# Seven first products of the feed-forward's first row group run as fill of the last attention group, with their Mish behind the seam

## The chip, the cores and the metric

The kernel runs on one core of one Trainium2 chip. The metric is the time of one execution in device microseconds; of the kernel before there are three runs, 677.23, 675.67 and 678.56 us, with 677.23 us as the median. In this document PE is TensorE's matmuls, PEld its weight loads, DVE is VectorE, ACT is ScalarE, POOL is GpSimd, and SP is the queue that issues all DMAs of this kernel.

## What is computed

One transformer block with adaptive layer norm on one sequence of 2048 rows: sliding-window attention (16 heads of 28 columns, a window of 256), then a two-layer feed-forward with Mish between its layers. Everything is in float32.

```python
B, S, D, F, H, W = 1, 2048, 448, 1792, 16, 256
mod = (silu(c) @ w_mod).reshape(c.shape[0], 6, 1, -1)
sa, ca, ga, sb, cb, gb = (mod[:, i] for i in range(6))
h = layernorm(x) * (1 + ca) + sa
q, k, v = heads(h @ wqkv)
p = softmax(where(0 <= i - j < W, q @ k.T * 28 ** -0.5, -1e9))
x = x + ga * ((p @ v) @ wo)
h = layernorm(x) * (1 + cb) + sb
x = x + gb * (mish(h @ w1 + b1) @ w2)
```

## The kernel before

**Split operands.** A float32 factor is kept as a high part, rounded for the fast matmul format, and a low part, the rest. A product of two such factors is three matmuls for each 128 rows of the contraction: high by high, high by low, low by high. With 448 rows (three chunks of 128 and one of 64, which holds its own low part in the other 64 partitions) one product of the first layer is 11 matmuls (`passes`, L205). ACT makes a high part as a copy, DVE or POOL the low part as a difference.

**Row groups.** The 2048 rows are four groups of 512. The attention runs over 4 groups x 16 heads x 3 blocks of the band, 192 steps `u` of the loop at L1109, so steps 144 to 191 are the last group. A step issues B(u): on PE the scores of one head and block into one of two PSUM banks `sB` (after a bfloat16 matmul, L759, that adds the mask, unless ACT has put the mask there ahead of time, L739, a "seed"), and on ACT their exponential `P` (L734). Every fourth step issues `pv`, 16 narrow matmuls (L769). Most steps also issue a scan of the scores of a later head, `sA` on PE with a masked maximum `junk` on DVE (L687, L689), up to step 179.

**Fill.** The order of the work on every engine is the order of the program text; nothing reorders it. So each step also pulls other work from generators and issues it between the attention's own: `fill_main(g)` (L994) by a credit of RATE[g] per step against a cost for each piece of matmul work, and one `side_step` per step from `fill_late` (in the last group: `gen_w1`, L841). Evictions of such work are put in `pipe` and issued one or two steps later. In the last group the fill was the output projection of the group before (`gen_oT`, then `gen_wo`: 44 matmuls `wo`), and then the second layer norm of row group 0 (`gen_ln2_0`: four ACT normalisations `x`, 16 transposes `trf`, four evictions `hhf` on ACT and their low parts on DVE). RATE was 0.45. `gen_w1` loaded and split 4 of the 16 pieces of W1. When the steps are over, the generators are drained (L1152).

**The seam and the feed-forward.** At steps 192 to 195 (`TAIL`) the first two products z0 and z1 of the feed-forward start beside the last `pv`, and ACT loads the table that holds Mish. Then the loop at L1213 goes over 4 row groups x 14 column blocks, n = 0 to 55. Loop n issues `f1_mm(n)` (11 matmuls `z`, L970), `f1_act(n)` (on ACT Mish `t` and its high part `ah`, on DVE its low part `al`, L976 to L978), in row group 0 `pieces(n)` (ACT and POOL split the n-th piece of W2 into `w2h` and `w2l`, and pieces of W1), and `ff2(n - 1)` (12 matmuls `acc`, L1177 to L1179, of which every third needs `al`). In row group 0 four `fill_step`s per loop issue the rest of the attention's work: transposes and projection of the last group (`ot`, `wo`, with DVE's additions `xr`) and the second layer norm of row group 1, whose 64 transposes run on DVE (`yt`, L897, four blocks of 16). z14, the first product of row group 1, needs all of them. `ah` and `al` have two buffers each.

Of the kernel before, what the change touches and what calls it, by code (L numbers as in the profile page):

```python
# [51 lines left out]
def adaln_block(ctx: ExitStack, tc: tile.TileContext, x, wqkv, wo, w1, b1, w2, c, w_mod, out):  # L52
# [582 lines left out]
    def gen_wo(g, tag, bufs):  # L635
        oh, ol = OT[g]

        def add(xr, p, t):
            DVE.tensor_tensor(xr, xr, p[:, 0:D], op=ALU.add)
            ln_stats(xr, mv2[g][:, t, :], cst, f"w{g}{t}")  # L640

        xrs = XR[g]

        def store(xr, t):
            j = 4 * g + t
            dma(x1d[j * 128:(j + 1) * 128, :], xr)
            if t == 0:
                later.append(lambda: xr_load(g, 3))

        for t in range(4):  # L650
            j = 4 * g + t
            if t not in xrs:
                flush()
            xr = xrs[t]
# [25 lines left out]
    def A(i, t):  # L680
# [5 lines left out]
        p = bank("mm" if i >= 60 and t % 2 else "sA", 2, f"sA{i}_{t}")  # L686
# [115 lines left out]
    FW = {}  # L802
# [6 lines left out]

    def w2_dma(f):  # L810
        w2p[f] = load_piece(w2[f * 128:(f + 1) * 128, :], 0, 0, D, stage(f"w2p{f}"))
# [23 lines left out]
    SEQ = [e for f in range(NF) for e in [("w2", f)] + [("w1", n) for n in (2 * f + 4, 2 * f + 5) if n < len(W1)]]  # L835
# [5 lines left out]
    def gen_w1():  # L841
# [12 lines left out]
        w1_load(0)  # L854
        for n in range(1, 4):
            yield
            yield
            w1_load(n)
        yield "bank"
        b1c = FW["b1c"] = p1.tile([128, NF], F32, name="b1c")  # L860
        p = bank("mm", 2, "b1t")
        PE.transpose(p[:, 0:NF], b1r, ident[0:NF, 0:NF])
        ACT.activation(b1c, p[:, 0:NF], AF.Copy)
        x1_load(0, p1)
# [6 lines left out]
        yield "bank"  # L871
        pb = bank("mm", 2, "gb")
# [3 lines left out]
        yield  # L876
# [27 lines left out]
    XN2 = {}  # L904

    def gen_ln2(g, pl, xn_tiles, tag, bufs):
        xs = None
        for r in gen_ln([x1[g][:, t, 0:D] for t in range(4)], pl, xn_tiles, f"f{g}", g == 0, mv=mv2[g]):
# [5 lines left out]
        if g:  # L914
            yield from ln2_blocks(g, xs, hh, hl)
            return
        for ci in range(4):
            p = bank(tag, bufs, f"trf{g}{ci}")
            tr_chunk(xs, ci, p)
            pipe.add(2, lambda p=p, ci=ci: hT_hi(p, ci, hh, 2), lambda p=p, ci=ci: hT_lo(p, ci, hh, hl, 2))  # L920
            yield
            yield

    def gen_ln2_0():
        p1 = FW["p1"]

        yield from gen_ln2(0, p1, lambda: [x1[0][:, t] for t in range(4)], "mm", 2)
        yield from finish()
        for i in range(4):
            piece_load(i)  # L930
            yield
# [10 lines left out]
    def pieces(f):  # L942
        for i, (kind, n) in enumerate(SEQ):
            if kind == "w2" and n == f:
                w2_split(n)
            elif kind == "w1" and (n - 4) // 2 == f:
                w1_hi(n)
                w1_lo(n, DVE if f < 1 else POOL)
            else:
                continue  # L950
# [9 lines left out]
    zb = {}  # L960

    def f1_mm(n, tag, part=(0, 11)):
        g, f = divmod(n, NF)
        hh, hl = h2[g]
        fs = slice(f * 128, (f + 1) * 128)
        if part[0] == 0:
            zb[n] = bank(tag, 2, f"z{n}")
        ps = passes(hh, hl, FW["w13"][:, :, fs], FW["w1l"][:, :, fs])
# [3 lines left out]
    def f1_act(n):  # L972
        f = n % NF
        ah[n], al[n] = ftile("ah", n, F32R), ftile("al", n, F32R)
        t = ftile("t", n)
        ACT.activation(t, zb[n], AF.Mish, bias=FW["b1c"][:, f:f + 1])  # L976
# [17 lines left out]
    def fill_main(g):  # L994
# [21 lines left out]
        if g + 1 == NG:  # L1016
            yield from finish()
            yield from gen_ln2_0()

# [29 lines left out]
    RATE = (0.76, 1.01, 0.88, 0.45)  # L1049
# [139 lines left out]
    def gen_x1_ln2(g):  # L1189
        if g > 1:  # L1190
            x1_load(g, (ff, p1)[g % 2])
# [9 lines left out]
    x1_load(0, ff)  # L1201
    for i in range(4, 9):
        piece_load(i)
    x1_load(1, p1)
# [8 lines left out]
    for n in range(NN + 1):  # L1213
        g, f = divmod(n, NF)
        if f == 0 and n:
# [42 lines left out]
```

## Time and profile before

| What | Value |
|---|---|
| Median of the three runs | 677.23 us |
| Lowest, highest | 675.67, 678.56 us |
| Span of the profiled execution, first to last instruction | 674.8 us |
| ACT busy over the span | 336.9 us (50%) |
| POOL busy over the span | 120.9 us (18%) |
| Mean granted TensorE clock of the span | 0.990 |

The profile gives no other time for the profiled execution than its span, which lies 0.9 us under the lowest of the three runs and 2.4 us under their median. Times in the trace are microseconds from the start of the span. The matmuls of the trace overlap (each record of 512 columns is about 0.4 us long, while the next one starts 0.23 us later), so a busy PE is not a full PE: the distance of one start from the next tells what a matmul costs, and the weight loads, one for each matmul of 128 columns of weights, show the pace.

### The profile page before, as it was taken

The numbers are of one execution on the slowest core, as the hardware profiler recorded it, in microseconds if no ns is written. First come the engines' busy times: TensorE is split into PE (matmuls) and PEld (weight loads), VectorE is DVE, ScalarE is ACT, GpSimd is POOL, SyncE is SP. The second block draws the span as 40 slices with busy tenths as digits, with TensorE's granted clock in tenths as the row PEclk, the third lists the DMA queues.
The fourth block names the chain that finished last, engine by engine and source line by source line (L and its number), as shares of the span: only waits on it lengthen the run. The fifth ranks groups of instructions, "written<-read, shape, count | busy, mean of one in ns | idle before, by whom it ended". The sixth has DMA issues, their size and how long they took to land.

```text
span 674.8 us, 10729 instructions
## 1 busy us (share of the span) xinstructions
PE 637.9 (95%) x3712; PEld 511.0 (76%) x3712; DVE 391.7 (58%) x1138; ACT 336.9 (50%) x584; POOL 120.9 (18%) x173
## 2 busy tenths in 40 slices
PE   4998999899999999998989999989999999999996
PEld 3876676577887678776666788878888888888885
DVE  6865676756677767567767333963485438631112
ACT  4554566678765677734667743442333323322221
POOL 6741010233011100000030245431012001100002
PEclk9999999999999999997999999999999999999999
DMA  8875775456855478434772654003000300010001
GB/s 227 225 234 191 263 260 159 134 149 197 279 138 156 140 220 289 144 107 113 192 217 63 220 162 137 14 1 110 0 1 0 109 2 0 1 54 1 1 0 54
DMA packets 49169, 83.77 MB, mean 124 GB/s; under 512 B 5838, under 2 KB 27612, under 8 KB 49116
## 3 DMA queue, kind: packets, MB, share of 16 engines
q1 hardware_dynamic: 49116, 83.10, 40.3%
q8 instruction: 29, 0.48, 0.3%
q14 instruction: 24, 0.20, 0.1%
HBM read 53.45 MB, written 29.36 MB: 123 GB/s over the span
## 4 chain that ended last, share of the span: by engine, by line
PE 66%; DVE 15%; issue 12%; DMA 3%; ACT 2%; POOL 1%; SPq 0%; POOLq 0%; DVEq 0%; ACTq 0%
PE z L970 15%; PE qk L321 8%; DVE junk L689 6%; PE sA L687 6%; PE pv L769 6%; PE sB L731 5%; PE acc L1179 4%; PE acc L1178 4%; PE acc L1177 4%; PE wo L321 3%; PE qk_v L321 3%; DVE yt L897 3%; PE sB L759 2%; DMA k<-scr 1%; PE qk L506 1%
## 5 line engine op out<-in xcount | busy, mean ns | idle before, releaser
L689 DVE CUSTOM_DVE_ANT_0 junk<-sA,strip 128x384 bf16<-128x384 f32 (+2 forms) x256 | 135.7, 530 | 91.6 <-PE sA L687 76.7
L734 ACT ACTIVATE P<-sB 128x512 f32<-128x512 f32 (+2 forms) x192 | 108.6, 571 | 99.1 <-PE sB L731 96.7
L978 DVE TENSOR_TENSOR al<-t,ah 128x512 fp32r<-128x512 f32 x56 | 41.2, 736 | 137.2 <-ACT ah L977 136.8
L976 ACT ACTIVATE t<-z,b1c 128x512 f32<-128x512 f32 x56 | 38.4, 686 | 156.8 <-PE z L970 145.8
L687 PE MATMUL sA<-k,q 84*128 84x384 f32 (+2 forms) x256 | 93.5, 370 | 10.7 <-DVE mx L689 6.2
L970 PE MATMUL z<-hhf,w 128*128 128x512 f32 x224 | 89.0, 397 | 0.0
L970 PE MATMUL z<-hlf,w 128*128 128x512 f32 x224 | 88.8, 396 | 0.0
L731 PE MATMUL sB<-q,k 86*128 86x384 f32 (+1 forms) x352 | 84.9, 316 | 0.0
L1179 PE MATMUL acc<-w2h,al 128*128 128x448 f32 x224 | 82.1, 366 | 1.9 <-DVE al L978 1.9
L1177 PE MATMUL acc<-w2h,ah 128*128 128x448 f32 x224 | 81.9, 366 | 0.0
L1178 PE MATMUL acc<-w2l,ah 128*128 128x448 f32 x224 | 81.8, 365 | 0.0
L731 PEld LDWEIGHTS sB<-q,k 86*128 86x128 f32 x352 | 59.4, 193 | 13.1 <-issue 5.1
L970 PE MATMUL z<-hhf,w1l 128*128 128x512 f32 x168 | 66.5, 396 | 0.0
L687 PEld LDWEIGHTS sA<-k,q 84*128 84x128 f32 x256 | 48.3, 191 | 23.2 <-DVE mx L689 15.1
L897 DVE STREAM_TRANSPOSE yt<-xn 32x128 f32<-32x128 f32 x192 | 58.1, 302 | 2.6
L739 ACT ACTIVATE sB<-strip 128x512 f32<-128x512 bf16 (+2 forms) x95 | 54.6, 575 | 3.0
L769 PE MATMUL pv<-P,v 128*32 128x256 f32 (+2 forms) x704 | 50.6, 402 | 0.0
L970 PEld LDWEIGHTS z<-hlf,w 128*128 128x128 f32 x224 | 42.1, 188 | 10.1
L970 PEld LDWEIGHTS z<-hhf,w 128*128 128x128 f32 x224 | 42.1, 188 | 9.1 <-issue 0.6
L1179 PEld LDWEIGHTS acc<-w2h,al 128*128 128x128 f32 x224 | 42.1, 188 | 5.9 <-DVE al L978 2.6
L1177 PEld LDWEIGHTS acc<-w2h,ah 128*128 128x128 f32 x224 | 42.1, 188 | 5.0
L1178 PEld LDWEIGHTS acc<-w2l,ah 128*128 128x128 f32 x224 | 42.1, 188 | 4.8
(155 smaller groups left out, 1024.2 us busy)
## 6 DMA issues: line engine op xcount, KB each, us to landing
k<-scr SPq DMA_DIRECT2D x48, 252.0 KB
q<-scr SPq DMA_DIRECT2D x64, 168.0 KB
scr<-st SPq DMA_DIRECT2D x21, 512.0 KB
scr<-st SPq DMA_DIRECT2D x29, 256.0 KB
x<-x1d SPq DMA_DIRECT2D x10, 448.0 KB
xin<-in_A_x_dram SPq DMA_DIRECT2D x8, 448.0 KB
xr<-in_A_x_dram SPq DMA_DIRECT2D x16, 224.0 KB
x1d<-xr SPq DMA_DIRECT2D x16, 224.0 KB
```

Source lines behind the costliest of these rows:

```text
L321: PE.matmul(p, b, a, start=(n == 0), stop=(n == 10))
L687: PE.matmul(p[:, c0:384], q[0:84, t * 128:(t + 1) * 128], k[0:84, t * 128 + c0:t * 128 + 384], start=True, stop=True)
L689: DVE.tensor_tensor_reduce(out=junk[:, c0:384], in0=p[:, c0:384], in1=mask[:, c0:384], scale=1.0, scalar=-3.0e38, op0=ALU.add, op1=ALU.max ...
L731: PE.matmul(p[:, c:c + 128 * (t1 - t0)], k[:, jj * 128:(jj + 1) * 128], q[:, t0 * 128:t1 * 128], start=False, stop=True, skip_group_check= ...
L734: ACT.activation(P[:, c0:], p[:, c0:], AF.Exp, scale=SCALE)
L739: ACT.activation(p[:, c0:], strip[:, c + c0:c + 512], AF.Copy)
L769: PE.matmul(pvb[q][32 * a:32 * a + 32, t0 * 128:t1 * 128], V[j % NV][:, h + a, :], Pt[4 * w + a][:, c:c + 128 * (t1 - t0)], start=(b == 0 ...
L897: DVE.transpose(y4[32 * j:32 * j + 32, ci, :, 32 * i:32 * i + 32], x4[32 * i:32 * i + 32, :, ci, 32 * j:32 * j + 32])
L970: PE.matmul(zb[n], ps[m][1], ps[m][0], start=(m == 0), stop=(m == 10))
L1177: PE.matmul(p, ah[n][:, ts], w2h[f], start=(f == 0), stop=False)
L1178: PE.matmul(p, ah[n][:, ts], w2l[f], start=False, stop=False)
L1179: PE.matmul(p, al[n][:, ts], w2h[f], start=False, stop=(f == NF - 1))
```

## The change

z2 to z8, the products of seven column blocks of row group 0, leave the feed-forward's loop and become the last item of the last attention group's fill (`gen_f1`). Their sums are moved from PSUM to SBUF by ACT, with the bias added (`z_out`), into three tiles `zs` of the tag `xr` and four slices `zx` of the tag `x1`. Behind the seam `f1_act` takes Mish in place from there. So that their operands are ready, W1's pieces 0 to 11 (before: 0 to 3) are loaded and split inside the last attention group, and the layer norm of row group 0 is done by `gen_w1` between those pieces instead of after the projection. The column blocks are taken in the order FO. RATE of the last group goes from 0.45 to 0.80. The last heads' scan uses two banks `sA` where it had four. Loads of the last group's `x` rows (`xr`) move behind the Mish that frees their buffers, and row group 0's residual `x1` is loaded a second time at loop n = 9.

```diff
-            if ci < 3:
+            if ci < 3 and g < NG - 1:
                 later.append(lambda t=ci: xr_load(g, t))
...
-        p = bank("mm" if i >= 60 and t % 2 else "sA", 2, f"sA{i}_{t}")
+        p = bank("sA", 2, f"sA{i}_{t}")
...
+    ZT = 2
+    ZN = 9
+    FO = (7, 8, 0, 1, 2, 3, 4, 5, 6, 9, 10, 11, 12, 13)
...
-    SEQ = [e for f in range(NF) for e in [("w2", f)] + [("w1", n) for n in (2 * f + 4, 2 * f + 5) if n < len(W1)]]
+    w1_cols = [0]
+    SEQ = [e for f in range(NF) for e in [("w2", f)] + [("w1", n) for n in (f + 11,) if 12 <= n < len(W1)]]
...
+        x1_load(0, p1)
+        for n in range(3):
             w1_load(n)
+            yield
+        ln = gen_ln([x1[0][:, t, 0:D] for t in range(4)], p1, lambda: [x1[0][:, t] for t in range(4)], "f0", True,
+                    mv=mv2[0])
...
-        for n in range(4):
+        for n in range(12):
+            next(ln, None)
             yield
             w1_hi(n)
-            yield "dve"
             w1_lo(n, POOL)
+            if n % 4 == 3:
+                w1_cols[0] += D
+            next(ln, None)
+            yield
+            if n == 2:
+                XN2[0] = [x1[0][:, t] for t in range(4)]
+            if n + 3 < 12:
+                later.append(lambda n=n: w1_load(n + 3))
...
+    def z_out(n, p):
+        if n < ZT + 3:
+            zs[n] = xr_tile(f"zs{n}")
+        else:
+            if n == ZT + 3:
+                FW["zx"] = FW["p1"].tile([128, 4, GT], F32, name="zx", tag="x1")
+            zs[n] = FW["zx"][:, n - ZT - 3]
+        f = FO[n]
+        ACT.activation(zs[n], p, AF.Identity, bias=FW["b1c"][:, f:f + 1])
...
+    def gen_f1():
+        for n in range(ZT, ZN):
+            while w1_cols[0] < 128 * (FO[n] + 1):
+                yield
+            p = bank("mm", 2, f"z{n}")
+            w = yield from tile_mms(p, f1_passes(n))
+            pipe.add(2, lambda n=n, p=p: z_out(n, p))
+            yield w
+        yield from finish()
...
-        t = ftile("t", n)
-        ACT.activation(t, zb[n], AF.Mish, bias=FW["b1c"][:, f:f + 1])
+        if n in zs:
+            t = zs[n]
+            ACT.activation(t, t, AF.Mish)
+        else:
+            t = ftile("t", n)
+            ACT.activation(t, zb[n], AF.Mish, bias=FW["b1c"][:, f:f + 1])
...
             yield from gen_ln2_0()
+            yield from gen_f1()
...
-    RATE = (0.76, 1.01, 0.88, 0.45)
+    RATE = (0.76, 1.01, 0.88, 0.80)
...
-    x1_load(0, ff)
+    x1_load(1, ff)
...
+        if n == ZN:
+            x1_load(0, p1)
...
-            f1_mm(n, "z")
+            if n not in zs:
+                f1_mm(n, "z")
             f1_act(n)
+        if n - ZT in (0, 1, 2):
+            xr_load(NG - 1, n - ZT)
```

**PE, attention step 183 to 184.** In the order of PE's instructions before, the step's fill is one group of transposes (`sB183` and `sB184` are the scores of steps 183 and 184, `et14` a transpose of the attention's output):

```order
L731 MATMUL sB183_4518<-q2_3_393,k3_7_381 128x384
L731 MATMUL sB183_4518<-q2_3_393,k3_7_381 128x128
L780 MATMUL et14_4525<-ident_127,o4_14_4491 128x128 x4
L254 MATMUL trf01_4530<-ident_127,x1_0_4150 128x128 x4
L759 LDWEIGHTS identr_136
L759 MATMUL sB184_4536<-strip_138,identr_136 128x256
```

In the order of the change, the same place on PE:

```order
L733 MATMUL sB183_4616<-q2_3_393,k3_7_381 128x384
L733 MATMUL sB183_4616<-q2_3_393,k3_7_381 128x128
L782 MATMUL et14_4623<-ident_127,o4_14_4591 128x128 x4
L321 MATMUL z5_4578<-hlf0_4257,w13_4008 128x512
L321 MATMUL z5_4578<-hhf0_4256,w13_4008 128x512
L321 MATMUL z5_4578<-hlf0_4257,w13_4008 128x512
L321 MATMUL z6_4631<-hhf0_4256,w13_4008 128x512
L321 MATMUL z6_4631<-hhf0_4256,w1l_4009 128x512
L761 LDWEIGHTS identr_136
L761 MATMUL sB184_4637<-strip_138,identr_136 128x256
```

The transposes are gone from here (they stand at steps 165 to 169 now), and five matmuls of z5 and z6 stand in their place. In the whole order of the change, steps 171 to 190 hold 70 of the 77 moved matmuls and step 191 the last 7; `wo` stands at 32 matmuls in steps 152 to 159 (19 before) and at 12 in steps 160 to 162 (25 in steps 160 to 171 before).

**ACT, attention steps 160 to 163.** Before, ACT's order holds the exponentials `P`, the seeds `sB` and, from step 163 on, a split of W1 (`w13`):

```order
L734 ACTIVATE P160_4082<-sB160_4049 128x512
L739 ACTIVATE sB162_4084<-strip_138 128x512
L734 ACTIVATE P161_4115<-sB161_4111 128x512
L734 ACTIVATE P162_4136<-sB162_4084 128x512
L739 ACTIVATE sB164_4138<-strip_138 128x512
L863 ACTIVATE b1c_4146<-b1t_4147 128x14
L734 ACTIVATE P163_4161<-sB163_4157 128x512
L186 ACTIVATE w13_3996<-w1p0_4000 128x448
```

In the change, the same steps on ACT:

```order
L736 ACTIVATE P160_4118<-sB160_4070 128x512
L741 ACTIVATE sB162_4120<-strip_138 128x512
L240 ACTIVATE x1_0_4012<-x1_0_4012,nmf0_4113,rsf0_4085 128x448
L736 ACTIVATE P161_4162<-sB161_4158 128x512
L186 ACTIVATE w13_4008<-w1p1_4028 128x448
L240 ACTIVATE x1_0_4012<-x1_0_4012,nmf0_4113,rsf0_4085 128x448
L736 ACTIVATE P162_4181<-sB162_4120 128x512
L741 ACTIVATE sB164_4183<-strip_138 128x512
L240 ACTIVATE x1_0_4012<-x1_0_4012,nmf0_4113,rsf0_4085 128x448
L736 ACTIVATE P163_4207<-sB163_4203 128x512
L186 ACTIVATE w13_4008<-w1p2_4055 128x448
L240 ACTIVATE x1_0_4012<-x1_0_4012,nmf0_4113,rsf0_4085 128x448
```

Four normalisations (they stood at steps 176 to 180 before) now lie in these four steps, and the four evictions `hhf` follow at steps 165 to 169 (before: 181 to 187).

**DVE, feed-forward loops 7 to 9.** In the change, DVE's order in the loops around the first two blocks of `yt1`, the transposes of row group 1's layer norm (`al7` is the low part of the Mish of block 7):

```order
L1015 TENSOR_TENSOR al7_5126<-zx_4635,ah7_5125 128x512
L913 STREAM_TRANSPOSE yt1_5136<-xn2_1_5091 32x4x32 x16
L1015 TENSOR_TENSOR al8_5166<-zx_4635,ah8_5165 128x512
L899 TENSOR_SCALAR yt1_5136<-yt1_5136,cols_182 128x512
L913 STREAM_TRANSPOSE yt1_5136<-xn2_1_5091 32x4x32 x16
L1015 TENSOR_TENSOR al9_5221<-t9_5222,ah9_5220 128x512
```

This order is that of before; only the source of `al7` and `al8` is another tile. On PE, the matmuls of z2 to z8 are missing between the `acc` of these loops.

More of the change, by code (lines that the diff above doesn't have):

```diff
@@ L808, in stage @@
         return stg(FW["p1"], name)
+    ZT = 2
+    ZN = 9
+    FO = (7, 8, 0, 1, 2, 3, 4, 5, 6, 9, 10, 11, 12, 13)
     def w2_dma(f):
-        w2p[f] = load_piece(w2[f * 128:(f + 1) * 128, :], 0, 0, D, stage(f"w2p{f}"))
+        w2p[f] = load_piece(w2[FO[f] * 128:(FO[f] + 1) * 128, :], 0, 0, D, stage(f"w2p{f}"))
     def x1_load(g, pl):
@@ L875, in gen_w1 @@
         ACT.activation(gbn, pb[:, 0:D], AF.Copy)
-        yield
+        for i in range(4):
+            piece_load(i)
+            yield
     def ln2_blocks(g, xs, hh, hl):
@@ L902, in blocks @@
                 yield
-    XN2 = {}
     def gen_ln2(g, pl, xn_tiles, tag, bufs):
         xs = None
-        for r in gen_ln([x1[g][:, t, 0:D] for t in range(4)], pl, xn_tiles, f"f{g}", g == 0, mv=mv2[g]):
+        for r in gen_ln([x1[g][:, t, 0:D] for t in range(4)], pl, xn_tiles, f"f{g}", mv=mv2[g]):
             xs = r or xs
@@ L945, in pieces @@
                 w2_split(n)
-            elif kind == "w1" and (n - 4) // 2 == f:
+            elif kind == "w1" and n - 11 == f:
                 w1_hi(n)
-                w1_lo(n, DVE if f < 1 else POOL)
+                w1_lo(n, POOL)
             else:
@@ L962, in f1_mm @@
     def f1_mm(n, tag, part=(0, 11)):
[L963 to L965 removed]
         if part[0] == 0:
             zb[n] = bank(tag, 2, f"z{n}")
[L968 removed]
+        ps = f1_passes(n)
         for m in range(*part):
```

48 lines of the change are left out of this document (22 added, 26 removed).

## Prediction

> **What bounds the kernel now.** I read the page's first table, then one table of the windows around the change, then the groups and instructions inside single windows.
>
> ```profile
> span 674.8 us, 10729 instructions
> PE 637.9 (95%) x3712; PEld 511.0 (76%) x3712; DVE 391.7 (58%) x1138; ACT 336.9 (50%) x584; POOL 120.9 (18%) x173
> PE 66%; DVE 15%; issue 12%; DMA 3%; ACT 2%; POOL 1%; SPq 0%; POOLq 0%; DVEq 0%; ACTq 0%
> ```
>
> PE is 95% busy and holds 66% of the chain that ended last, so the kernel is a matmul kernel with some idle places. Where they are, the windows tell. I cut them at attention steps 144, 152, 160 and 171, at z0's start (372.60), at the first block of DVE's transposes (422.40) and at z13's start (450.13); the last row is a full stretch for comparison, steps 60 to 71.
>
> ```profile
> core 0: us, PE busy (x) PEld busy (x) DVE busy (x) ACT busy (x) POOL busy (x), PEclk, DMA share, GB/s
> 302.30:318.00 15.70, 13.58 (x93) 9.54 (x93) 10.26 (x33) 7.41 (x14) 0.40 (x1) 0.78 0.51 144
> 318.00:330.50 12.50, 11.97 (x93) 9.03 (x94) 8.16 (x29) 7.00 (x13) 0.00 (x0) 1.00 0.42 128
> 330.50:348.00 17.50, 16.75 (x127) 11.41 (x126) 12.62 (x45) 12.05 (x23) 4.69 (x5) 1.00 0.78 214
> 348.00:372.60 24.60, 21.76 (x191) 14.60 (x190) 19.21 (x51) 17.16 (x31) 2.97 (x8) 0.93 0.36 110
> 372.60:422.40 49.80, 49.80 (x253) 42.74 (x252) 18.70 (x33) 25.00 (x44) 21.67 (x24) 1.00 0.57 176
> 422.40:450.13 27.73, 25.85 (x118) 21.66 (x117) 25.53 (x74) 12.14 (x19) 10.98 (x10) 1.00 0.04 9
> 145.60:168.20 22.60, 22.09 (x146) 17.00 (x145) 13.07 (x44) 18.52 (x35) 7.92 (x7) 1.00 0.69 218
> ```
>
> The reader is to see three things. From step 171 to the seam PE is thin: weight loads fill 14.60 of 24.60 us (59%), against 17.00 of 22.60 (75%) in the full stretch. From 372.60 to 422.40 PE has no idle at all. From 422.40 to 450.13 it is DVE that is full, 25.53 of 27.73 us.
>
> **The change part by part.** All sums are differences in the profiled execution, whose span of 674.8 us lies 2.4 us under the median of 677.23.
>
> *The feed-forward loses seven products.*
>
> ```profile
> 422.62 0.39 PE L970 MATMUL z<-hhf,w 128*128 128x512 f32 x1
> 425.19 0.36 PE L1177 MATMUL acc<-w2h,ah 128*128 128x448 f32 x1
> 427.64 0.39 PE L970 MATMUL z<-hhf,w 128*128 128x512 f32 x1
> ```
>
> From a z's first matmul to the first `acc` behind it are 425.19 - 422.62 = 2.57 us for 11 matmuls, 0.233 each; the 12 `acc` take 2.45 us, 0.204 each. Seven products are 18.0 us. Six of them (z2 to z7) stand before 422.40, where PE is dense: 6 x 2.57 = 15.4 us come off. The seventh, z8, starts at 422.62, behind DVE's first block, and there DVE sets the time:
>
> ```profile
> L897 DVE STREAM_TRANSPOSE yt<-xn 32x128 f32<-32x128 f32 x64 | 19.4, 302 | 0.8
> 441.60 0.47 PE L1179 MATMUL acc<-w2h,al 128*128 128x448 f32 x1 [0.79 <-DVE al L978]
> 447.98 0.47 PE L1179 MATMUL acc<-w2h,al 128*128 128x448 f32 x1 [1.09 <-DVE al L978]
> ```
>
> Already now PE waits twice for an `al` queued behind 16 transposes. The blocks keep their place in DVE's order, so z13 still follows the first block by some 27.7 us; taking z8 out of these lets PE arrive earlier and wait longer. **I count -15.4 us** and nothing for z8. Does something else become late where six z's leave? In loops 5 to 8 PE then does little but 2.45 us of `acc`. Behind them stand, for each loop:
>
> ```profile
> L186 ACT ACTIVATE w<-w1p 128x448 fp32r<-128x448 f32 x12 | 6.3, 568 | 0.5 <-DMA w1p<-in_B_w_dram 0.4
> L976 ACT ACTIVATE t<-z,b1c 128x512 f32<-128x512 f32 x8 | 5.5, 688 | 23.4 <-PE z L970 23.4
> L977 ACT ACTIVATE ah<-t 128x512 fp32r<-128x512 f32 x8 | 5.1, 632 | 0.3
> L939 ACT ACTIVATE w2h<-w2p 128x448 fp32r<-128x448 f32 x8 | 4.5, 565 | 0.0
> L940 POOL TENSOR_TENSOR w2l<-w2p,w2h 128x448 fp32r<-128x448 f32 x7 | 8.2, 1171 | 16.9 <-ACT w2h L939 9.9 <-DMA xr<-in_A_x_dram 6.0 <-POOL w L194 1.0
> L192 POOL TENSOR_TENSOR w1l<-w1p,w 128x448 fp32r<-128x448 f32 x7 | 8.0, 1156 | 0.0
> ```
>
> ACT 0.69 + 0.63 + 0.57 = 1.9 us, and 0.57 more in loops 1 to 4, where one W1 piece is left; POOL 1.17, and 1.16 more there. In loops 1 to 4 `ot` and `wo` lengthen PE's part, so ACT and POOL stay just under it, but without reserve. A moved piece's Mish no longer waits for PE. Bounds: -16.3 (the wait for z7's sum before `al7` goes as well) to -13 (the first loops lose half a microsecond each to ACT, POOL or a late `xr` load, and DVE's first block starts that much later).
>
> *Steps 152 to 159* take 32 `wo` instead of 19: 13 x 0.204 = 2.7 us, of which the window's 0.53 us of PE idle can hide a part. **+2.2 us**, between +1.0 and +3.0.
>
> *Steps 160 to 170* lose 12 `wo` (-2.4 us) and take 16 `trf`, on PE -0.7 us in all. ACT takes more. Its durations:
>
> ```profile
> L734 ACT ACTIVATE P<-sB 128x512 f32<-128x512 f32 x46 | 27.0, 597 | 29.1 <-PE sB L731 28.7
> L258 ACT ACTIVATE hhf<-trf,cols 128x512 fp32r<-128x512 f32 x4 | 3.1, 785 | 0.0
> L240 ACT ACTIVATE x<-x,nmf,rsf 128x448 f32<-128x448 f32 x4 | 3.0, 753 | 0.0
> 359.35 1.07 ACT L734 ACTIVATE P<-sB 128x512 f32<-128x512 f32 x2
> ```
>
> Four `hhf` (3.1), four `x` (3.0) and one more W1 piece (0.57) on top of 12.05 us busy are 18.7 us, in a window of 17.50. Two activations in a row take 1.07 where one takes 0.60, so a queue that never starves would need some 10% less, about 17 us; at the highest share that a window here shows (18.52 of 22.60, 82%) it would be 22.8 us. I take 19.0, nearer to the full queue since the added activations need nothing that is late. **+1.5 us**, from -0.7 (PE alone) to +5.3.
>
> *Steps 171 to 191* take the 77 matmuls (18.0 us) and lose the 16 `trf`. What a step of attention takes when PE is full comes from the last window: its groups are
>
> ```profile
> L321 PE MATMUL qk<-hl,wq 128*128 128x512 f32 x19 | 7.6, 403 | 0.0
> L321 PE MATMUL qk<-hh,wq 128*128 128x512 f32 x19 | 7.6, 401 | 0.0
> L687 PE MATMUL sA<-k,q 84*128 84x384 f32 x16 | 5.7, 356 | 0.0
> L321 PE MATMUL qk<-hh,wql 128*128 128x512 f32 x14 | 5.5, 392 | 0.0
> L759 PE MATMUL sB<-strip,identr 128*128 128x256 bf16 (+1 forms) x30 | 5.9, 263 | 0.0
> L687 PE MATMUL sA<-k,q 84*128 84x384 f32 x12 | 4.3, 400 | 1.2 <-DMA k<-scr 1.1
> ```
>
> (the first four of 145.60 to 168.20, the last two of 348.00 to 372.60). 52 fill matmuls of 512 columns are 52 x 0.233 = 12.1 us of the 22.60; 10.5 us are left for 12 steps, 0.87 a step with all its small waits. 21 such steps are 18.4 us. They would hold 28 scans `sA`; here are 12, and 16 fewer at 0.175 (384 of 512 columns) are -2.8. The full stretch has no mask matmuls; here are 30, mostly in pairs that delay the scores by 0.10 (an estimate from
>
> ```profile
> 359.05 0.34 PE L759 MATMUL sB<-strip,identr 128*128 128x128 bf16 x2
> 359.15 0.48 PE L731 MATMUL sB<-q,k 86*128 86x384 f32 x2
> ```
>
> ): +1.5. With `gb` (0.4) and the 18.0 us of z: 18.4 - 2.8 + 1.5 + 0.4 + 18.0 = 35.5 us, against 24.60 now: **+10.9 us**. Some 5.4 us of the 16.3 us of net new matmuls (18.0 - 1.7) thus vanish in idle time. Below: +9.5, if the steps without `sA` have no wait left. Above: +14, if PE's order, in which a late score still stops the z's behind it, closes only 2 us of the idle.
>
> Hidden, at zero: ACT's seven evictions `zs` and `zx` (each like an `hhf`, under 0.8 us) in steps of some 1.7 us that hold 0.6 of `P`; POOL's eight more W1 pieces (1.16 each) in a stage where it is busy 2.97 of 24.60; DMA (share 0.36 there, though 0.78 in the window before; 1.8 MB more, at 214 GB/s some 9 us of transfer over 45 us); the second `x1` load, behind all W2 loads in SP's queue. If that cover fails, z's wait for weights inside PE's queue, and the scores behind them too.
>
> Sum: 2.2 + 1.5 + 10.9 - 15.4 = -0.8 us, that is 677.23 - 0.8 = **676.4 us**.
>
> One rule of the Trainium skill speaks on how much idle there is to fill. Its page "Trainium Kernel Development and Optimization", section "Performance Expectations", calls matmul busy time a bad metric, since matmuls are pipelined, and weight-load busy a good one. By PE's busy row the stage from step 171 has 24.60 - 21.76 = 2.8 us to fill, and the sum would be +1.8 us instead of -0.8. The rows above (59% against 75% weight loads) agree with the page.
>
> **The rivals.** *Everything fits* (faster): ACT runs as a full queue in steps 160 to 170 (-0.7) and the late steps lose their waits (+9.8): 2.2 - 0.7 + 9.8 - 15.6 = -4.3, 672.9 us. For it: ACT waited 28.7 us for scores in the group's row above, so it has time for more if the work comes early. Against: its additions come bunched, 1.9 us a step in steps 160 to 163, and exponentials wait behind them.
>
> *ACT becomes the bound* (slower): in steps 160 to 170 ACT's order puts `x`, `w` and `hhf` ahead of exponentials for which `pv` and the next scores wait. Above about 1.6 us of ACT a step it decides, as PE needs that much with fill; steps 160 to 163 reach 1.92 (0.60 + 0.57 + 0.75). At the 82% share, 22.8 us: 2.2 + 5.3 + 11.5 - 15.4 = +3.6, 680.8 us. Against: PE's fill there is thin, so a late exponential costs little at first.
>
> *The feed-forward gives less back* (slower): ACT, POOL and SP were covered by 2.57 us of z a loop; without it each of seven loops loses about 0.6: 2.2 + 1.5 + 10.9 - 11.2 = +3.4, 680.6 us. In the rows ACT and POOL need at most 2.5 us in loops 1 to 4.
>
> *The clock.* In the fourth window the granted clock is 0.93: 24.60 x 0.07 = 1.7 us at half speed are lost in a stretch where PE stood idle. My 35.5 us, built from a window with clock 1.00, count that dip as gone; if it stays, the sum is +0.9, still no change. The dip of the first window (0.78) lies ahead of all that changes.
>
> The Trainium skill's page "TensorE: Matmul & The Clock Gate", section "HAM oscillation", has the array fall to half clock after about 3.4 us of idle; by it a fuller PE has no dip from step 171, as I assume, and by the other reading the sum is the +0.9. No trace here shows yet which.
>
> **How the numbers follow.** A measurement of this kernel tells about 0.5%, 3.4 us, from no change. No change (-0.8, with its own range 673.9 to 680.6): 0.46. Faster, the first rival and what lies below: 0.32. Slower: 0.22 (ACT 0.13, the feed-forward 0.09). The range for 8 in 10 goes from -4.7 (all of the first rival and a little) to +4.3 (either slower rival and a little): **672.5 to 681.5 us**.
>
> **What would show it.** In the changed profile: z2 to z8 between steps 171 and 191, in a stage from step 171 to z0 of 35 to 36 us at clock 1.00 (37 or more: waits stayed); steps 160 to 170 in 19 us with ACT almost full (17: everything fits; 22: ACT bound); z0 to z13 in 62 us instead of 77.5, with PE's waits for `al` at four places instead of two (65 or more: the loops starve). I am wrong if z's wait in PE's queue for W1's pieces, or if another dip of the clock shows.

## The result and the profile after

The changed kernel takes 681.97 us (median of five runs, 681.16 to 683.79) beside 675.99 us for the kernel before (five runs, 674.84 to 678.56): a ratio of 1.0077, with a 95% interval of 1.0050 to 1.0104. It is slower, by about 6 us, where -0.8 us was predicted. The profiled execution took 681.16 us, 1.8 us more than its span; the sums below are in spans.

The page's head for the changed kernel, and its chain of waits by engine:

```profile
span 679.4 us, 10742 instructions
PE 640.9 (94%) x3712; PEld 511.5 (75%) x3712; DVE 389.7 (57%) x1136; ACT 341.1 (50%) x591; POOL 123.5 (18%) x175
PE 65%; DVE 14%; issue 12%; DMA 3%; ACT 3%; SPq 1%; POOL 1%; POOLq 0%; DVEq 0%; ACTq 0%
```

Almost nothing is seen in it: 4.6 us lost in 680 do not show in shares of the span. The windows do. They are cut in the changed kernel at the same events as the prediction's: steps 144, 152, 160, 171, z0's start, DVE's first block of transposes, z13's start.

```profile
core 0: us, PE busy (x) PEld busy (x) DVE busy (x) ACT busy (x) POOL busy (x), PEclk, DMA share, GB/s
304.62:317.23 12.61, 10.54 (x93) 7.54 (x92) 10.06 (x33) 7.34 (x14) 1.65 (x3) 1.00 0.62 176
317.23:334.65 17.42, 16.60 (x128) 12.88 (x128) 10.84 (x38) 7.75 (x14) 0.00 (x0) 1.00 0.49 155
334.65:357.06 22.41, 16.58 (x116) 11.81 (x108) 14.21 (x42) 17.16 (x31) 8.06 (x12) 0.85 0.56 162
357.06:392.80 35.74, 35.19 (x248) 24.43 (x248) 14.35 (x45) 19.98 (x37) 6.89 (x6) 1.00 0.37 100
392.80:427.81 35.01, 34.53 (x184) 29.90 (x183) 18.27 (x32) 20.85 (x37) 15.14 (x16) 1.00 0.58 181
427.81:454.90 27.09, 24.34 (x109) 19.97 (x108) 24.72 (x74) 11.48 (x19) 11.26 (x12) 1.00 0.15 48
```

| Term | Before | Changed | Difference | Predicted |
|---|---|---|---|---|
| Steps 152 to 159 | 12.50 | 17.42 | +4.9 | +2.2 |
| Steps 160 to 170 | 17.50 | 22.41 | +4.9 | +1.5 |
| Steps 171 to z0 | 24.60 | 35.74 | +11.1 | +10.9 |
| z0 to the end of the span | 302.2 | 286.6 | -15.6 | -15.4 |

The two large terms are right to 0.2 us each, and z0 to z13 is the 62.1 us that was forecast. The two small ones, together +3.7, came out at +9.9; how this splits between the two rows hangs on the mark of step 160, as the experiments show. Ahead of step 152 the two executions differ too, by 2.3 us up to step 144, where no instruction differs, and by -3.1 us in steps 144 to 151 (12.61 for 15.70, at a clock of 1.00 for 0.78). Both go with stretches of half clock that fell in other places. Of the 2.3 us, 2.2 arise in steps 36 to 59 (39.1 us for 36.9), where of the two only the changed kernel ran at half clock, in this window:

```profile
119.70:130.00 10.30, 9.94 (x55) 6.20 (x53) 5.27 (x19) 5.63 (x9) 0.94 (x1) 0.50 0.24 75
```

What stands in those 40 us? On ACT, in order of time, around step 159 (in brackets the idle time before the instruction and what ended it):

```profile
331.08 0.60 ACT L736 ACTIVATE P<-sB 128x512 f32<-128x512 f32 x1 [0.95 <-PE sB L733]
334.17 0.58 ACT L186 ACTIVATE w<-w1p 128x448 fp32r<-128x448 f32 x1 [2.49 <-DMA w1p<-in_B_w_dram]
334.65 0.58 ACT L736 ACTIVATE P<-sB 128x512 f32<-128x512 f32 x1
```

ACT stands 2.49 us in front of the first W1 piece, with an exponential queued behind it. Beside it, instructions of PE in the same kernel, in order of time:

```profile
334.00 1.07 PE L771 MATMUL pv<-P,v 128*32 128x128 f32 x16
336.36 0.40 PE L733 MATMUL sB<-q,k 86*128 86x256 f32 x2
340.33 0.41 PE L689 MATMUL sA<-k,q 84*128 84x384 f32 x1 [3.57 <-DMA k<-scr]
344.67 1.94 PE L771 MATMUL pv<-P,v 128*32 128x256 f32 x16
386.77 1.07 PE L771 MATMUL pv<-P,v 128*32 128x256 f32 x16
```

PE waits 3.57 us for a head's K, and the next 16 `pv` behind it take 1.94 us, where 16 of the same shape take 1.07 at 386.77. The windows cut around the wait say why:

```profile
334.65:342.00 7.35, 3.78 (x27) 2.95 (x20) 3.55 (x12) 5.31 (x10) 3.34 (x7) 0.97 0.74 214
342.00:348.40 6.40, 5.66 (x32) 3.50 (x30) 3.67 (x13) 3.69 (x7) 1.32 (x2) 0.50 0.56 165
348.40:357.06 8.66, 7.14 (x61) 5.37 (x59) 6.98 (x19) 8.16 (x15) 3.40 (x3) 1.00 0.41 114
```

Soon behind the wait, from 342.00 on, the granted clock is 0.50 for 6.4 us. So two things may cost time here: the wait, and a stretch at half speed behind it. And why is K late? SP's issues, first in the kernel before, then in the changed one:

```profile
327.13 0.37 SPq L59 DMA_DIRECT2D x1d<-xr  x1
328.01 0.38 SPq L59 DMA_DIRECT2D k<-scr  x1
329.71 0.39 SPq L59 DMA_DIRECT2D k<-scr  x1
331.58 0.36 SPq L59 DMA_DIRECT2D xr<-in_A_x_dram  x1
333.28 1.04 SPq L59 DMA_DIRECT2D x<-x1d  x2
```

```profile
326.65 0.90 SPq L59 DMA_DIRECT2D x<-x1d  x2
327.60 0.46 SPq L59 DMA_DIRECT2D w1p<-in_B_w_dram  x1
328.10 0.43 SPq L59 DMA_DIRECT2D x1d<-xr  x1
328.63 1.00 SPq L59 DMA_DIRECT2D w1p<-in_B_w_dram  x2
334.75 0.33 SPq L59 DMA_DIRECT2D xr<-in_A_x_dram  x1
335.59 0.38 SPq L59 DMA_DIRECT2D k<-scr  x1
336.91 0.38 SPq L59 DMA_DIRECT2D k<-scr  x1
```

The fourth `xr` load of row group 2 takes the buffer of the first row tile, so SP must wait until the store `x1d` of that tile has landed. Before, the load stood behind both K loads. Now `wo` runs at nearly twice the pace, its first tile is stored earlier in the program, and the load stands ahead of both: SP issues nothing from 329.6 to 334.75. SP's waits of the changed kernel in steps 152 to 170, in total, times, longest:

```profile
SPq L59 <- DMA x1d<-xr: 5.0, 1, 5.0
```

Around the store 0.9 MB of `x1` and three pieces of W1 are in transfer as well; which of the two, the place in the queue or the burst, makes K late is for the experiments.

### The profile page after: what moved, and what is told of

Its sections match the earlier page's. It is cut to its first block, busy times and chain, and to the rows that moved or that the text cites. A ratio compares the mean times of both kernels' runs of the same rounds, so it can differ in the third digit from the quotient of the medians.

```text
span 679.4 us, 10742 instructions
## 1 busy us (share of the span) xinstructions
PE 640.9 (94%) x3712; PEld 511.5 (75%) x3712; DVE 389.7 (57%) x1136; ACT 341.1 (50%) x591; POOL 123.5 (18%) x175
## 4 chain that ended last, share of the span: by engine, by line
PE 65%; DVE 14%; issue 12%; DMA 3%; ACT 3%; SPq 1%; POOL 1%; POOLq 0%; DVEq 0%; ACTq 0%
PE z L1003 12%; PE qk L321 9%; PE sA L689 6%; PE pv L771 6%; DVE junk L691 5%; PE sB L733 5%; PE acc L1217 4%; PE acc L1216 4%; PE acc L1215 4%; PE wo L321 3%; PE qk_v L321 3%; DVE yt L913 3%; PE z L321 2%; PE sB L761 2%; DMA k<-scr 1%
## 5 line engine op out<-in xcount | busy, mean ns | idle before, releaser
L1015 DVE TENSOR_TENSOR al<-t,ah 128x512 fp32r<-128x512 f32 x49 | 35.5, 725 | 123.2 <-ACT ah L1014 122.8
L1013 ACT ACTIVATE t<-z,b1c 128x512 f32<-128x512 f32 x49 | 33.7, 688 | 129.6 <-PE z L1003 118.7
L1003 PE MATMUL z<-hhf,w 128*128 128x512 f32 x196 | 78.0, 398 | 0.0
L1003 PE MATMUL z<-hlf,w 128*128 128x512 f32 x196 | 77.7, 397 | 0.0
L689 PEld LDWEIGHTS sA<-k,q 84*128 84x128 f32 x256 | 48.9, 192 | 24.0 <-DVE mx L691 15.6
L1003 PE MATMUL z<-hhf,w1l 128*128 128x512 f32 x147 | 58.2, 396 | 0.0
L1003 PEld LDWEIGHTS z<-hlf,w 128*128 128x128 f32 x196 | 36.8, 188 | 8.8
L1003 PEld LDWEIGHTS z<-hhf,w 128*128 128x128 f32 x196 | 36.9, 188 | 8.2 <-issue 0.8
```

Source lines behind the costliest of these rows:

```text
L689: PE.matmul(p[:, c0:384], q[0:84, t * 128:(t + 1) * 128], k[0:84, t * 128 + c0:t * 128 + 384], start=True, stop=True)
L1003: PE.matmul(zb[n], ps[m][1], ps[m][0], start=(m == 0), stop=(m == 10))
```

## The experiments

Theory 1 was that K (and W1) come late, through SP's queue and the burst of transfers. Rival 2 was the prediction's own "ACT becomes the bound": four normalisations and three W1 pieces bunched in steps 160 to 163. Rival 3 was that the half clock falls by chance, and nothing else. Each kernel is the changed one with the edit shown; ratios are to the kernel before, timed beside it.

| Run | us | Ratio, 95% interval | Steps 152-159, 160-170 |
|---|---|---|---|
| the change | 681.97 | 1.0077 (1.0050 to 1.0104) | 17.4, 22.4 |
| e1_xr4 | 679.06 | 1.0047 (1.0015 to 1.0080) | 17.8, 19.3 |
| e2_pool | 682.90 | 1.0096 (1.0067 to 1.0125) | 15.5, 25.5 |
| e3_both | 678.81 | 1.0035 (1.0013 to 1.0057) | 15.3, 22.7 |
| e4_noz | 690.78 | 1.0203 (1.0180 to 1.0227) | 17.3, 23.2 |
| e5_w1late | 677.12 | 0.9992 (0.9967 to 1.0017) | 15.5, 20.3 |
| e6_w1mid | 678.26 | 1.0007 (0.9983 to 1.0031) | 15.3, 19.7 |
| e7_w1late_xr3 | 680.64 | 1.0036 (1.0011 to 1.0061) | 15.7, 22.3 |
| e8_rate | 680.91 | 1.0055 (1.0035 to 1.0075) | 13.8, 20.3 |
| e9_late_pool | 678.22 | 1.0007 (0.9992 to 1.0021) | 15.4, 19.4 |
| e10_z8 | 676.64 | 0.9996 (0.9976 to 1.0017) | 15.3, 19.9 |
| e11_z8r | 677.30 | 0.9997 (0.9977 to 1.0018) | 15.4, 20.3 |
| e12_order | 682.82 | 1.0073 (1.0047 to 1.0099) | 15.3, 21.3 |

### One cause at a time: the queue, or ACT

A fourth buffer for `xr`, so that nothing waits for the store:

```diff
-        return mid.tile([128, 512], F32, name=name, tag="xr", bufs=3)
+        return mid.tile([128, 512], F32, name=name, tag="xr", bufs=4)
...
-            if ci < 3 and g < NG - 1:
+            if (ci < 3 or g == 2) and g < NG - 1:
...
-            if t == 0:
+            if t == 0 and g != 2:
                 later.append(lambda: xr_load(g, 3))
```

> The changed kernel with a fourth buffer for the residual rows xr, so that the fourth xr load of row group 2 is issued early and no longer stands in SP's queue waiting 5.0 us for the store of the first row tile; K and Q loads behind it go out at once. Nothing else is changed. Theory 1 (SP's queue, blocked behind that load, makes K late; PE idles 3.57 us, and the clock falls to half from 341.6 to 348.4): the wait for K goes, the dip goes with it, steps 152 to 170 fall from 39.9 us to 33 to 35, the time by 4 to 7 us, to 675 to 678. Rival 2 (ACT's added work in steps 160 to 163 is the bound): the wait for K goes but ACT's order keeps the stage at 38 to 40 us, time 680 to 682. Rival 3 (the dips of the clock come by chance): the wait goes, a dip of 6.8 us stands elsewhere in the group, time 678 to 680.

The high parts of W1's first four pieces on POOL:

```diff
-            w1_hi(n)
+            split_hi(w1p[n], FW["w13"][:, W1[n][0], W1[n][1]:W1[n][1] + D], POOL if n < 4 else ACT)
```

> The changed kernel with the high parts of the first four W1 pieces made on POOL instead of ACT, so that ACT does not wait for the first W1 piece (2.49 us there now) and has 4 x 0.57 us less to do in steps 158 to 163. Theory 1 (K late through SP's queue is what costs): ACT's wait goes, the 3.57 us wait for K and the dip stay, time 680 to 682. Rival 2 (ACT is the bound in steps 158 to 163): steps 152 to 170 fall from 39.9 us by 3 to 6, time 676 to 679.

Both edits:

> Both edits: a fourth xr buffer, and the first four W1 pieces' high parts on POOL. Theory 1: little better than the fourth buffer alone, 674 to 677. Rival 2: as the POOL edit alone or better by the K wait, 674 to 677 too, but then the buffer alone does not reach it. If both waits are needed for the loss, only this one falls to 676 or below.

e1_xr4's windows of steps 152 to 159 and 160 to 170:

```profile
316.57:334.38 17.81, 17.00 (x129) 12.91 (x130) 11.26 (x40) 7.75 (x15) 0.00 (x0) 1.00 0.56 175
334.38:353.66 19.28, 15.02 (x112) 11.18 (x108) 13.84 (x42) 16.97 (x32) 8.08 (x12) 0.91 0.61 171
```

The first row of PE's waits in them (total, times, longest):

```profile
PE sA L689 <- DMA k<-scr: 2.1, 1, 2.1
```

The same two views of e2_pool, windows first:

```profile
317.80:333.30 15.50, 14.72 (x107) 11.62 (x108) 9.16 (x32) 7.26 (x13) 0.00 (x0) 1.00 0.45 139
333.30:358.80 25.50, 19.77 (x131) 14.25 (x129) 15.88 (x48) 15.94 (x27) 10.18 (x16) 0.80 0.55 166
```

and PE's longest wait, and its `pv` between the scores of steps 160 and 161:

```profile
PE sA L689 <- DMA k<-scr: 3.7, 1, 3.7
334.54 1.07 PE L771 MATMUL pv<-P,v 128*32 128x128 f32 x16
```

e2 is the reading to remember. ACT's wait for W1 is gone, and steps 152 to 159 look 1.9 us shorter, but on PE nothing moved: from the mark of step 152 to that `pv` it takes 334.00 - 317.23 = 16.77 us in the changed kernel and 334.54 - 317.80 = 16.74 us here. The stages are cut at ACT's exponentials, and in the changed kernel the exponential of step 160 stands behind ACT's wait; the wait delays the mark and not PE. So 1.9 us of the row "Steps 152 to 159" belong to the row "Steps 160 to 170". PE then waits 3.7 us for K as before, and the time is not better at all. (ACT's wait is not simply gone either: POOL, which now splits W1, is late with `nmf`, and ACT stands 2.7 us in front of the first `x` for it.) e1 shortens the wait for K to 2.1 us, not to zero: SP no longer waits for the store, yet the transfer is late among the others. In time its median is about 3 us lower, less than the 4 to 7 expected; its runs spread from 677 to 687 us, and by the intervals it isn't told from the changed kernel. The windows of the one profile of each (37.1 us in place of 39.8) show the gain. e3, with both, lies by e1 rather than at the 676 or below that "both waits are needed" would have given, and W1's three pieces still travel ahead of K in it.

### The preparations without the products

```diff
-    ZN = 9
+    ZN = 2
```

> The changed kernel with its seven products z2 to z8 left where they were, in the feed-forward; all the preparations stay (more fill per step, early layer norm, twelve W1 pieces in the group, order of the blocks). Theory 1 and rival 2 both put the loss into steps 152 to 170, ahead of the first of these products: 39.9 us there as in the changed kernel, 24 to 26 us from step 171 to z0 instead of 35.7, and the rest 15 to 16 us longer: 685 to 687. If the moved products themselves cost more than they give, it is below 682.

The windows of steps 152 to 159, 160 to 170, and 171 to z0 in e4_noz:

```profile
317.40:334.70 17.30, 16.73 (x128) 12.85 (x128) 10.99 (x38) 7.75 (x15) 0.00 (x0) 1.00 0.50 155
334.70:357.90 23.20, 17.18 (x112) 12.42 (x108) 14.04 (x42) 16.99 (x31) 8.06 (x12) 0.78 0.56 161
357.90:383.90 26.00, 21.84 (x170) 14.03 (x170) 14.35 (x45) 15.43 (x30) 6.80 (x6) 0.87 0.51 134
```

The loss stands in steps 152 to 170, as in the changed kernel, without a single moved product. From step 171 to z0 it is 26.0 us, and z0 to the end is 686.2 - 383.9 = 302.3: the products themselves give 15.7 us back for 9.7, a gain. The median of 690.78 us lies 4 us over the expected range, and the profiled execution (688.09 us) 1 us over it; the other four took 690 to 692 at granted clocks of 0.968 to 0.976 (0.986 in the profiled one). So part of the miss goes with time at half clock; where it fell in those four no profile shows.

### The burst of transfers

W1's loads and splits begin four steps later (e5, with the fourth `xr` buffer), two steps later (e6, the same buffer), and four steps later with three buffers (e7). The core of it for e5:

```diff
         x1_load(0, p1)
         for n in range(3):
-            w1_load(n)
             yield
...
-        for n in range(12):
+        for n in range(-2, 12):
             next(ln, None)
             yield
+            if n < 0:
+                w1_load(n + 2)
+                next(ln, None)
+                yield
+                continue
```

> The changed kernel with the fourth xr buffer, and with the loads of W1 begun four steps later, so that only the x1 tile (0.9 MB) and not three W1 pieces (0.67 MB) as well lie ahead of the K and Q loads of steps 158 and 160; the splits of W1 follow four steps later too. Layer norm, transposes and the moved products keep their steps. If it is the burst of transfers that makes K late (theory 1, in the wider form that the queue's block and the share of the DMA engines both count): the wait for K falls below 0.7 us from 2.10, no dip of the clock in steps 160 to 170, steps 152 to 170 take 32 to 34 us (37.1 with the buffer alone, 39.8 in the changed kernel), time 673 to 676. If ACT's bunched work is the bound after all, steps 160 to 163 lose W1's splits only: 36 to 38 us, 678 to 680. If dips come by chance, one stays in the group and the time is 676 to 679.

e6 differs from e5 by:

```diff
-        for n in range(-2, 12):
+        for n in range(-1, 12):
...
-                w1_load(n + 2)
+                w1_load(0)
                 next(ln, None)
                 yield
+                w1_load(1)
                 continue
...
-            if n == 0:
+            if n == 1:
                 XN2[0] = [x1[0][:, t] for t in range(4)]
```

> As e5_w1late, with the loads and splits of W1 begun two steps later instead of four. By the burst: between the two, 33 to 36 us in steps 152 to 170, 674 to 678; less left over at the seam than with four steps.

e7 differs from e5 by the three buffers of the change, with its order of the `xr` loads:

```diff
-        return mid.tile([128, 512], F32, name=name, tag="xr", bufs=4)
+        return mid.tile([128, 512], F32, name=name, tag="xr", bufs=3)
```

> W1 begun four steps later, but with three xr buffers as in the changed kernel, so that SP still waits for the store of the first row tile ahead of the K loads. If the queue's block alone decides, the wait for K stays near 3.6 us with a dip, and the time at 680 to 682. If the burst decides, the store lands sooner (the W1 pieces are not in its way), SP waits 1 to 3 us instead of 5.0, K is late by under 2 us, and the time is 675 to 679.

The windows of steps 152 to 159 and 160 to 170 in e5_w1late:

```profile
318.10:333.56 15.46, 14.77 (x107) 11.64 (x108) 9.19 (x32) 7.25 (x14) 0.00 (x0) 1.00 0.53 149
333.56:353.89 20.33, 18.72 (x131) 14.19 (x129) 15.79 (x48) 16.97 (x29) 5.43 (x8) 0.83 0.63 183
```

The first row of PE's waits in them (two more are of 0.3 us):

```profile
PE sA L689 <- DVE mx L691: 1.8, 4, 1.2
```

In e7_w1late_xr3, SP's wait for the store:

```profile
SPq L59 <- DMA x1d<-xr: 5.9, 1, 5.9
```

and PE's for K:

```profile
PE sA L689 <- DMA k<-scr: 2.8, 1, 2.8
```

With both edits there is no wait for K at all, and the kernel is level with the one before (0.9992), 0.85% better than the change as it was made. Each edit alone (1.0047, 1.0036) gives a third to a half of that by the medians. e7 also corrects a detail of theory 1: W1's pieces were not what delayed the store, since SP waits for it 5.9 us without them. What W1's lateness takes away is ACT's wait and part of the burst ahead of K.

e5 also parts the wait from the half clock. Its second window has as much half clock as the changed kernel's (a clock of 0.83 over 20.33 us, 0.85 over 22.41), and steps 152 to 170 are still 4.0 us shorter (35.8 for 39.8), about the wait for K of 3.57. e6's second window, at clock 1.00, takes 19.68 us; so the stretch of half clock is worth some 0.7 us here (W1 starts two steps apart in the two), and what the changed kernel loses more is mainly the wait. The stretch came in e5 without any long wait, so a long wait is not the only thing that brings it; whether it falls by chance, as rival 3 says, one profile of each kernel doesn't show.

### Rival 2 once more, with the transfers in time

e5_w1late with the edit of e2:

```diff
-            w1_hi(n)
+            split_hi(w1p[n], FW["w13"][:, W1[n][0], W1[n][1]:W1[n][1] + D], POOL if n < 4 else ACT)
```

> e5_w1late with the high parts of the first four W1 pieces made on POOL instead of ACT. With the transfers no longer late, rival 2 (ACT's bunched work in steps 160 to 163) gets its clean test: if ACT is the bound there, 4 x 0.57 = 2.3 us of its work leave and steps 160 to 170 fall from 20.3 us by 1.5 to 2.5, time 674.5 to 676; if not, the time stays at 677 within 1 us, and POOL's added work costs nothing or a little.

Its windows of steps 152 to 159 and 160 to 170:

```profile
316.96:332.38 15.42, 14.76 (x107) 11.64 (x108) 9.20 (x32) 7.27 (x14) 0.00 (x0) 1.00 0.49 150
332.38:351.81 19.43, 15.55 (x130) 11.37 (x129) 16.46 (x48) 15.11 (x26) 7.56 (x12) 1.00 0.63 183
```

ACT is 1.9 us less busy (15.11 us for 16.97), and the window is 0.9 us shorter at a clock of 1.00 instead of 0.83; beside e6, also at 1.00 and with all of ACT's work, it is 0.25 us shorter. The time is the same (1.0007). ACT is not the bound of these steps.

### Other divisions of the fill, and the place of one load

e5_w1late with half a unit of fill per step up to step 163 and 0.95 behind:

```diff
+            if g == 3:
+                RATE[3] = 0.5 if v < 20 else 0.95
             credit += RATE[g] * (2 if v < FRONT[g] else 1)
```

> e5_w1late (fourth xr buffer, W1 four steps later) with the fill spread otherwise: half a unit per step instead of 0.80 in steps 144 to 163, 0.95 behind, so that wo again fills steps 152 to 166 (21 matmuls up to step 159, as before the change had 19) and the seven products stand in steps 173 to 191. If steps 152 to 159 cost 15.3 to 15.5 us instead of 12.5 only by the 13 matmuls of wo moved there, and steps 160 to 170 had idle time for them: 13 to 13.5 and 19.5 to 20.5, together 1 to 2.5 us less, time 674.5 to 676.5, under the kernel before. If the stage is bound by something else (the chain of scores and exponentials), the sum of the two stays at 35 to 36 us and the time at 677.

e8_rate's windows of steps 152 to 159, 160 to 170, and 171 to the first `acc`:

```profile
319.50:333.30 13.80, 12.64 (x96) 9.53 (x97) 8.11 (x28) 7.14 (x14) 0.00 (x0) 1.00 0.55 161
333.30:353.60 20.30, 17.12 (x137) 12.72 (x136) 15.65 (x52) 16.10 (x29) 5.47 (x8) 1.00 0.66 186
353.60:401.60 48.00, 46.59 (x300) 32.23 (x299) 19.67 (x48) 26.81 (x47) 9.17 (x8) 0.93 0.39 108
```

The first two windows did what was expected, 1.7 us less together than in e5, and the third gave back more: it takes 48.0 us (43.2 in e5, 353.9 to 397.1). The products are pressed into fewer steps there, and the window has a clock of 0.93, 3.4 us lost at most; which of the two makes the 4.8 us isn't separated. By the ratios the kernel is 0.6% worse than e5.

e5_w1late with six products moved instead of seven:

```diff
-    ZN = 9
+    ZN = 8
```

> e5_w1late with six of the seven products moved: the seventh, the prediction's z8, stays in the feed-forward, where the prediction counted nothing for taking it out because DVE's transposes set the time there. If that holds, steps 171 to z0 lose up to 11 x 0.233 = 2.6 us (2.0 to 2.6, as PE is full there) and the feed-forward gives back 15 to 16 us all the same: 674.5 to 676. If z8 does cover something in the feed-forward (PE would have had it for nothing there), the feed-forward is 1.5 to 2.6 us longer and the time 677 within 1 us.

and that with less fill per step behind step 171:

```diff
+            if g == 3:
+                RATE[3] = 0.80 if v < 27 else 0.69
```

> e10_z8 with 0.69 units of fill per step instead of 0.80 from step 171 on, so that the six products last up to step 191 instead of ending at step 190 a little early. By the sums of the prediction nothing or up to 0.5 us less than e10_z8; if evenly spread fill hides more of it in the waits of the scores, 1 us less.

The feed-forward's z by line, first in e5_w1late; the two times behind the durations are the first start, that of z0, and the last:

```profile
L1009 PE MATMUL z<-hhf,w x196: 391/394/741, 389.6 to 664.3; 128*128 128x512 f32 x196
```

and in e10_z8:

```profile
L1009 PE MATMUL z<-hhf,w x200: 391/394/741, 386.5 to 662.0; 128*128 128x512 f32 x100
```

Step 171 to z0 is 386.5 - 353.3 = 33.2 us, 2.5 less than in e5; z0 to the end is 673.4 - 386.5 = 286.9, 0.9 more than e5's 675.6 - 389.6 = 286.0. But the kernels with seven products moved spread from 285.9 to 286.8 us there (e7 took 286.8), so the 0.9 isn't told from nothing, and leaving z8 where it was is worth 1.6 to 2.5 us in the profile. In time e10 and e5 aren't told apart (0.9996 and 0.9992), nor is e11, and none of them beats the kernel before beyond its interval.

Last, e7's three buffers, with the fourth `xr` load put behind the K and Q loads in SP's order:

```diff
-                later.append(lambda: xr_load(g, 3))
+                (hold if g == 2 else later).append(lambda: xr_load(g, 3))
...
+        if u == 160:
+            hold.pop()()
```

> W1 begun four steps later and three xr buffers, as in e7_w1late_xr3, but the fourth xr load of row group 2 is put behind the K and Q loads of steps 158 and 160 in SP's order, where it stood in the kernel before; it still waits for the store of the first row tile. If the place of that load in SP's queue is what made K late (and not the number of buffers), the wait for K is gone as in e5_w1late, steps 152 to 170 take 34.5 to 36 us and the time is 676 to 678 (e5_w1late: 677). If the burst of transfers alone did it, or DVE's addition that waits for the later xr load holds the scans of the scores up, the K wait or a wait of DVE stays and the time is 679 to 681 as with e7_w1late_xr3.

PE's longest wait in steps 152 to 170 of e12_order:

```profile
PE sA L691 <- DVE mx L693: 3.1, 4, 2.4
```

and DVE's for `xr`:

```profile
DVE xr L641 <- DMA xr<-in_A_x_dram: 1.2, 1, 1.2
```

The wait for K is gone, and a new one has come: DVE's addition stands 1.2 us in front of the later `xr`, the maxima of the scores queue behind it, and PE waits 2.4 us for one of them. So the place in SP's queue is what made K late in e7, and changing it alone is not enough: at the pace of 0.80 three buffers are too few in both places that were tried. Its median of 682.82 us is worse than this profile (span 676.8) accounts for; its runs spread from 678 to 684, and why is open.

## Why the prediction was wrong

**The step that failed** is the line "Hidden, at zero: ... DMA (share 0.36 there, though 0.78 in the window before; ...)". It weighed transfers by bytes over the stage from step 171, where there was room, and not by their place in SP's queue in steps 156 to 160, where the change puts `x1`, three W1 pieces and the `xr` load ahead of two heads' K and Q. The runs show its price: PE waits 3.57 us for one K, and steps 152 to 170 take 39.8 us, where they take 35.0 to 35.8 without that wait (e5, e6). This order stood in the program before anything ran; the part on the change went through PE, ACT and DVE, and not through SP. The price of the cover failing was named for the wrong place: "z's wait for weights inside PE's queue". No z waited for weights; the scan `sA` of a later head, which stands in PE's order ahead of the scores of step 163 and of the fill behind it, waited for K. The condition "or if another dip of the clock shows" did come true.

**Steps 152 to 159, +2.2, and 160 to 170, +1.5**: measured +4.9 each by the marks, but 1.9 us of the first is the late mark of step 160, so it is about +3.0 and +6.8. With the transfers in time and the clock at 1.00, and all of ACT's work in place, they are +2.8 and +2.2 (e6: 15.33 for 12.50, 19.68 for 17.50). Both are inside their bounds (1.0 to 3.0, -0.7 to 5.3); together the terms are 1.3 us too small for the work itself and lack 4.8 us for what comes late.

**Steps 171 to z0, +10.9**: +11.1. The count of 0.87 us per step without fill and 0.233 per matmul held; so did the reading of the stage by weight loads. The rule of the page "Trainium Kernel Development and Optimization", section "Performance Expectations", in the Trainium skill led the right way here: by PE's busy row there were 2.8 us to fill; 5.4 were counted, and 16.3 - 11.1 = 5.2 found. **The feed-forward, -15.4**: -15.6. The seventh product, counted at nothing, gives 0 to 0.9 us (e10 against the others). PE waits for `al` at three places there, 2.4 us in all, where four places were forecast.

**The rivals.** "ACT becomes the bound" gave 22.8 us for steps 160 to 170 and 680.8 us, and 22.4 and 682 were measured. That it was right in place and size is luck, since its cause is wrong: taking 2.3 us of work off ACT gained nothing, either in the changed kernel (e2) or with the transfers in time (e9). "The feed-forward gives less back" and "everything fits" did not happen.

**The clock.** The dip of step 171 and later is gone at 1.00, as assumed, and a new one came at steps 163 to 165. The Trainium skill's page "TensorE: Matmul & The Clock Gate", section "HAM oscillation", has the array fall to half clock after about 3.4 us of idle. The changed kernel's 3.57 us agree with it (the half clock begins 1.3 us behind that wait's end); e1's window is at 0.91 after a wait of 2.1 us, and e5's at 0.83 with no wait over 1.2 us, so here the wait's length is not the condition by itself.

What stays open: the pace of 0.80 was not undone alone in the changed kernel, with its three buffers and early W1, so how much of the store's wait is the pace and how much the burst of `x1` is not separated. The 4.0 us of the windows are also less than the 0.85% (5.8 us) between the medians of e5 and the changed kernel; where the rest lies isn't shown.

With the cover restored, the whole change is worth -0.08% (e5; interval -0.33% to +0.17%), where -0.8 us, or -0.12%, was forecast. That fits the sum for a kernel whose transfers arrive, which this one's did not; the interval is too wide to confirm it.

## What to carry to other kernels

When a change moves loads, read the order of the issuing queue beside the orders of the engines: a transfer that waits for a buffer holds every transfer behind it, whatever the share of the DMA engines says. When fill is drawn forward, count its buffers again for the new pace; with three, SP waited 1.4 us for the store at 0.45, and 5.0 us at 0.80. And a wait on one engine is a cost only if the engine that bounds the stage is later for it: compare that engine's own instructions, and not a mark on the waiting one. ACT's 2.5 us moved a mark by 1.9 us and PE by nothing. When one cure gains less than expected, look at what the wait became before dropping the theory: for K, two cures had to come together.

## What the runs showed of the hardware

Stretches of half clock are a cost of their own, and vary from run to run. Of the kernel before, 111 runs timed beside these experiments took 674.8 to 683.5 us at mean granted clocks of 0.994 to 0.975; twice the missing clock times the span is 8 to 34 us at half speed, and a straight line through them gives 0.24 us of time for each us of it. So a profile of one execution may carry a dip that another does not, and a difference of 2.3 us ahead of the first changed instruction (as here, up to step 144) is no effect of the change. The price depends on the place: steps 144 to 151 of the changed kernel and the twelve made from it took 12.4 to 12.9 us in the nine profiles without half clock there, 14.0 and 14.2 in the two with 3.4 us of it, and 15.6 in the two with 6.8, some 0.45 us for each us; in steps 160 to 170 it was some 0.1 (e5 against e6).

Transfers that go out early still slow each other: e1 issued that K at 329.89, ahead of any wait for the store, and PE had it only at 338.24, after a wait of 2.1 us. The Trainium skill's page "DMA: Bandwidth & Descriptors", section "Issuing engines are not separate DMA queues", says that all issuers' transfers run on the same 16 engines and interleave, and that a second issuer saves only the sequencer's time, usually small. No run here issues from a second engine, so neither is tested; the 5.0 us for which SP stood in the changed kernel were a wait, not time to issue.
